# A grouped 1x1 convolution on one core: five chunk stores split into 112 rows and four times four rows

## The chip, the core and the metric

The kernel runs on one core of a Trainium2 chip. The core has compute engines with queues of their own: TensorE (PE, with its weight loads shown as PEld), VectorE (DVE), ScalarE (ACT) and GpSimd (POOL). SyncE (SP) issues DMAs. Sixteen DMA engines, numbered 0 to 15, move data between HBM and the on-chip memory SBUF; TensorE writes its results to PSUM. Work is ordered by semaphores, which an instruction or a finished DMA raises and another instruction waits for.

The metric is the time of one execution on the device in microseconds. A comparison of this kernel can tell differences of about 0.5%.

## The reference

The input x is an image of 512 x 512 pixels with 192 channels in bfloat16, the weights w are 1 x 1 x 4 x 48 x 48. The channels are in four groups of 48, and within a group each pixel's 48 values are multiplied by that group's 48 x 48 matrix:

```python
G, Cg = 4, 48
xg = x.reshape(B, H, W, G, Cg)
out = jnp.einsum('bhwgc,gcd->bhwgd', xg, w[0, 0])   # k is 1, so one tap and no padding
return out.reshape(B, H, W, 192)
```

It reads 100.66 MB of x and writes 100.66 MB of output.

## The kernel before

The 262,144 pixels are cut into 33 chunks. The first 28 and three of the tail have 64 pixels per partition, the last two have 32 (`PPC`, `TAIL`). A chunk of 64 lies as 128 rows, one per SBUF partition, and each row is a contiguous run of 64 x 192 bfloat16 values (24,576 bytes) in HBM. `rows_view` (L101) gives this view of input and output, so that a chunk is loaded by one DMA and stored by one DMA of 3072 KB. Four buffers hold loaded chunks (`x_sb`) and four hold chunks to be stored (`o_sb`, `NB` = 4); chunk n uses buffer n % 4.

SyncE issues the loads (L156). The load of chunk n waits until TensorE has transposed all of chunk n - 4 (`t_done`, L155).

TensorE works on groups of four pixels per partition, sixteen groups to a chunk of 64. For a group it makes six transposes into PSUM (L188) and six matmuls (L210) with a block-diagonal arrangement of the weights that is built once at the start (L174, L232). Before the first group of a chunk it takes 16 from the load's semaphore (L184), which a load raises to 16 when it has landed. The transposes run `LOOK` = 2 groups ahead of the matmuls. Most groups run inside a hardware loop over four chunks at a time; the five tail chunks are written out.

VectorE copies each group's transposes from PSUM to SBUF (L238), and in five groups of sixteen (`SHARE`) also one half of the matmul results (L245). ScalarE copies the matmul results, whole (L279) or the other half (L276), into `o_sb`. Both wait, before their first result of chunk n, for the complete store of chunk n - 4 (L242, L268), since it reads the same buffer. The amount waited for is taken from `st_total`, which counts 16 for each store DMA on that buffer's semaphore.

ScalarE also issues the stores, from its own queue and in program order with its copies. When a chunk's last copy is made, the store is put on the list `pending`, and it is issued two groups later (one in the tail) by `store` (L255 to L263). At the end ScalarE waits for all stores (L286).

Of the kernel before, what the change touches and what calls it, by code (L numbers as in the profile page):

```python
# [11 lines left out]
C = GROUPS * CG  # L12
# [12 lines left out]
PPC = 64  # L25
NB = 4
TAIL = (64, 64, 64, 32, 32)
NXP = 4
NOB = 4
NXS = 4  # L30
# [18 lines left out]
def shared(g):  # L49
    return (g % PERIOD) in SHARE  # L50


def bass_standalone__grouped__vision_kernel(nc, x, w, out):
# [4 lines left out]
    per_part = npix // 128  # L58
    mid = per_part - sum(TAIL)
    assert mid > 0 and mid % (NB * PPC) == 0  # L60
    n_mid = mid // PPC
    trips = n_mid // NB
    sizes = [PPC] * n_mid + list(TAIL)
    n_chunks = len(sizes)

    xf = x.rearrange("b h w c -> (b h w) c")
    of = out.rearrange("b h w c -> (b h w) c")
# [14 lines left out]
    body = NB * PPC // 4  # L82
    assert body % NXP == 0 and body % PERIOD == 0 and L1 == body * trips
    assert not shared(-1) and not shared(-2)
# [10 lines left out]
    def actT_cnt(g):  # L95
        return g - GT + 1

    def dveT_cnt(g):
        return sum(1 for h in range(GT, g + 1) if shared(h))

    def rows_view(ap, n):  # L101
        s = sizes[n]
        return ap[pix0[n]:pix0[n] + 128 * s, :].rearrange("(p i) c -> p (i c)", p=128)

    st_total, acc = [], [0] * NB
    for n in range(n_chunks):
        acc[n % NB] += 16
        st_total.append(acc[n % NB])

    def st_before(n):  # L110
        return st_total[n - NB] if n >= NB else 0

    with ExitStack() as es:
        block = es.enter_context(nc.Block())
        x_sb = [es.enter_context(nc.sbuf_tensor(f"x_sb{i}", [128, PPC * C], BF16)) for i in range(NB)]
        o_sb = [es.enter_context(nc.sbuf_tensor(f"o_sb{i}", [128, PPC * C], BF16)) for i in range(NB)]
# [4 lines left out]
        wt = es.enter_context(nc.sbuf_tensor("wt", [128, WCOLS], BF16))  # L121
        xT_ps = es.enter_context(nc.psum_tensor("xT_ps", [128, NXP, 1024], BF16))
        o_ps = es.enter_context(nc.psum_tensor("o_ps", [128, NOB, 512], F32))

        def sem(name):
            return es.enter_context(nc.semaphore(name))

        ld_sem = [sem(f"ld{i}") for i in range(NB)]
        st_sem = [sem(f"st{i}") for i in range(NB)]
# [6 lines left out]
        @block.gpsimd  # L136
        def _(gp):
            gp.memset(esel[:], 1.0).then_inc(p0_sem, 1)  # L138
            gp.memset(ident[:], 1.0).then_inc(p1_sem, 1)  # L139
            gp.wait_ge(p0_sem, 1)  # L140
            gp.affine_select(out=esel[:], in_=esel[:], pattern=[[-1, ECOLS]],  # L141
                             compare_op=AluOpType.is_equal, fill=0.0, base=ESHIFT,
                             channel_multiplier=1).then_inc(e_sem, 1)
            gp.wait_ge(p1_sem, 1)
            gp.affine_select(out=ident[:], in_=ident[:], pattern=[[-1, 128]],  # L145
                             compare_op=AluOpType.is_equal, fill=0.0, base=0,
                             channel_multiplier=1).then_inc(id_sem, 1)
# [13 lines left out]
        def _(pe):  # L161
# [16 lines left out]
            def transposes(g):  # L178
# [7 lines left out]
                for j in range(6):  # L186
                    col = lg * 2 * UC + j * 128
                    last = pe.transpose(xT_ps[:, g % NXP, j * 128:(j + 1) * 128],  # L188
                                        x_sb[b][:, col:col + 128], ident[:])
# [39 lines left out]
        def _(dve):  # L229
# [4 lines left out]
            for (op, g) in dve_prog:  # L234
                n, lg = groups[g]
                if op == "ev1":
                    wq.wait(t_done, g + 1)
                    dve.tensor_copy(xT_sb[g % NXS][:], xT_ps[:, g % NXP, 0:2 * UC]).then_inc(ev1_sem, 1)  # L238
                else:
# [9 lines left out]
        @block.scalar  # L249
        def _(act):  # L250
            wq = Waiter(act)
            act.sem_inc(act_sem, 2)
            pending = []

            def store(n):  # L255
                b = n % NB
                g = g1[n] - 1
                if g < GT:
                    wq.wait(mm_done, g + 3)
                else:  # L260
                    wq.wait(actT_sem, actT_cnt(g))
                    wq.wait(ev2T_sem, dveT_cnt(g))
                act.dma_start(rows_view(of, n), o_sb[b][:, 0:sizes[n] * C]).then_inc(st_sem[b], 16)  # L263

            for g in range(NG):
                n, lg = groups[g]
                if lg == 0:
                    wq.wait(st_sem[n % NB], st_before(n))  # L268
                wq.wait(mm_done, g + 1)
                while pending and pending[0][1] <= g:  # L270
                    store(pending.pop(0)[0])
                v = (2 * g) % NOB
                ob = o_sb[n % NB]
                if shared(g):
                    u = lg * 2
                    ins = act.copy(ob[:, u * UC:(u + 1) * UC], o_ps[:, v, 0:UC])  # L276
                else:
                    dst = ob[:, lg * 2 * UC:(lg + 1) * 2 * UC].rearrange("p (u c) -> p u c", u=2)
                    ins = act.copy(dst, o_ps[:, v:v + 2, 0:UC])  # L279
                ins.then_inc(act_sem if g < GT else actT_sem, 1)  # L280
                if g == g1[n] - 1:
                    pending.append((n, g + 2 if g < GT else g + 1))
            for (n, _) in pending:
                store(n)
            for b in range(NB):
                act.wait_ge(st_sem[b], acc[b])  # L286
# [28 lines left out]
```

## Time and profile before

| What | Value |
|---|---|
| Runs | 491.99, 489.92 and 491.54 us; median 491.54 |
| Profiled execution, its own time | 492.02 us |
| Span of that execution, first to last instruction | 490.3 us |
| Mean granted TensorE clock | 0.956 |
| Chunk loads: 31 of 3072 KB and 2 of 1536 KB, first and last issue | 0.8 and 426.2 us |
| Chunk stores: 31 of 3072 KB and 2 of 1536 KB, first and last issue | 31.4 and 474.0 us |
| One issue of a store on ScalarE's queue, median | 338 ns |
| Store, issue to landing, least / median / most | 15.9 / 40.3 / 45.6 us |
| Load, issue to landing, least / median / most | 10.0 / 38.4 / 45.6 us |

The profile shows one execution. The span runs from the first to the last instruction that was recorded. "Busy" counts an engine's own work and leaves out waiting and issuing. The DMA share is the mean busy share of the sixteen DMA engines, and GB/s is what they moved together in a stretch, counted by packets that start in it. A wait names the instruction that waited, what released it, and the microseconds. PEq is TensorE's sequencer: L165 there is the place where it takes from a semaphore. A DMA counts as landed when its last DMA engine has reported.

### The profile page before, as it was taken

The numbers are of one execution on the slowest core, as the hardware profiler recorded it, in microseconds if no ns is written. First come the engines' busy times: TensorE is split into PE (matmuls) and PEld (weight loads), VectorE is DVE, ScalarE is ACT, GpSimd is POOL, SyncE is SP. The second block draws the span as 40 slices with busy tenths as digits, with TensorE's granted clock in tenths as the row PEclk, the third lists the DMA queues.
The fourth block names the chain that finished last, engine by engine and source line by source line (L and its number), as shares of the span: only waits on it lengthen the run. The fifth ranks groups of instructions, "written<-read, shape, count | busy, mean of one in ns | idle before, by whom it ended". The sixth has DMA issues, their size and how long they took to land. (4 is left out here: it accounts for less than half of the span.)

```text
span 490.3 us, 14833 instructions
## 1 busy us (share of the span) xinstructions
PE 416.1 (85%) x6154; PEld 402.6 (82%) x6154; DVE 349.4 (71%) x673; ACT 348.8 (71%) x513; POOL 1.3 (0%) x8
## 2 busy tenths in 40 slices
PE   0987898999999999979897998977997979979850
PEld 0976798999999999979887888877987879979740
DVE  0766677888888888868676776766885767858740
ACT  1676687888888888867675776766785767858650
POOL 1000000000000000000000000000000000000000
PEclk9999899999999999999898998999998999989985
DMA  8999999999999999999999999999999999999760
GB/s 354 429 404 429 428 419 430 433 425 437 426 437 428 433 429 433 430 433 429 431 428 431 429 435 428 433 429 433 431 430 431 432 431 433 426 430 432 305 286 39
DMA packets 9736, 201.65 MB, mean 411 GB/s; under 512 B 1264, under 2 KB 1264, under 8 KB 1264
## 3 DMA queue, kind: packets, MB, share of 16 engines
q1 hardware_dynamic: 4960, 100.68, 48.2%
q10 hardware_dynamic: 4752, 100.67, 48.0%
q8 instruction: 13, 0.21, 0.2%
q14 instruction: 11, 0.09, 0.0%
HBM read 100.68 MB, written 100.66 MB: 411 GB/s over the span
## 5 line engine op out<-in xcount | busy, mean ns | idle before, releaser
L279 ACT CAST o_sb<-o_ps 128x768 bf16<-128x768 f32 x352 | 274.5, 798 | 114.2 <-PE o_ps L210 76.0
L238 DVE COPY xT_sb<-xT_ps 128x768 bf16<-128x768 bf16 x512 | 283.9, 554 | 87.9 <-PE xT_ps L188 79.1
L210 PE MATMUL o_ps<-wt,xT_sb 128*128 128x144 bf16 (+1 forms) x3072 | 305.9, 237 | 39.9 <-PEq L165 29.0
L188 PE MATMUL xT_ps<-ident,x_sb 128*128 128x128 bf16 x3072 | 263.5, 224 | 6.0 <-issue 4.0
L210 PEld LDWEIGHTS o_ps<-wt,xT_sb 128*128 128x128 bf16 x3072 | 216.0, 99 | 52.3 <-issue 37.2
L188 PEld LDWEIGHTS xT_ps<-ident,x_sb 128*128 128x128 bf16 x3072 | 203.7, 100 | 6.9 <-issue 6.6
L245 DVE CAST o_sb<-o_ps 128x384 bf16<-128x384 f32 x160 | 88.5, 553 | 23.3 <-DMA out_dram<-o_sb 20.5
L276 ACT CAST o_sb<-o_ps 128x384 bf16<-128x384 f32 x160 | 76.6, 479 | 10.1 <-PE o_ps L210 6.4
L174 PE MATMUL o_ps<-w_sb,esel 48*128 48x48 bf16 x10 | 0.6, 211 | 11.1 <-DMA w_sb<-in_w_dram 11.1
L174 PEld LDWEIGHTS o_ps<-w_sb,esel 48*128 48x128 bf16 x10 | 0.5, 113 | 11.1 <-issue 11.1
L232 DVE CAST wt<-o_ps 128x480 bf16<-128x480 f32 x1 | 0.7, 657 | 11.7 <-PE o_ps L174 11.7
L279 ACT ACT_TABLE_LOAD x1 | 1.3, 1283 | 0.9 <-PEq L300 0.9
L141 POOL TENSOR_SCALAR_AFFINE_SELECT esel<-esel 48x272 bf16<-48x272 bf16 x1 | 0.4, 405 | 0.0
L138 POOL MEMSET esel<- 48x272 bf16 x1 | 0.3, 318 | 0.3 <-POOLq L300 0.3
L145 POOL TENSOR_SCALAR_AFFINE_SELECT ident<-ident 128x128 bf16<-128x128 bf16 x1 | 0.3, 285 | 0.0
L139 POOL MEMSET ident<- 128x128 bf16 x1 | 0.2, 198 | 0.0
L300 POOL MEMSET const-bfloat16-1.0<- 128x1 bf16 x1 | 0.1, 101 | 0.0
L300 POOL MEMSET const-uint8-127<- 128x1 uint8 x1 | 0.1, 101 | 0.0
L300 POOL MEMSET const-float32-0.0<- 128x1 f32 x1 | 0.1, 98 | 0.3 <-issue 0.3
L300 POOL MEMSET const-float32-1.0<- 128x1 f32 x1 | 0.1, 98 | 0.0
## 6 DMA issues: line engine op xcount, KB each, us to landing
x_sb<-in_x_dram SPq DMA_DIRECT2D x31, 3072.0 KB, 38.2
out_dram<-o_sb ACTq DMA_DIRECT2D x31, 3072.0 KB, 40.7
x_sb<-in_x_dram SPq DMA_DIRECT2D x2, 1536.0 KB, 39.4
out_dram<-o_sb ACTq DMA_DIRECT2D x2, 1536.0 KB, 17.3
w_sb<-in_w_dram SPq DMA_DIRECT2D x1, 18.0 KB, 9.8
```

The costliest lines, as they stand in the source:

```text
L138: gp.memset(esel[:], 1.0).then_inc(p0_sem, 1)
L141: gp.affine_select(out=esel[:], in_=esel[:], pattern=[[-1, ECOLS]], compare_op=AluOpType.is_equal, fill=0.0, base=ESHIFT, channel_multipli ...
L145: gp.affine_select(out=ident[:], in_=ident[:], pattern=[[-1, 128]], compare_op=AluOpType.is_equal, fill=0.0, base=0, channel_multiplier=1) ...
L174: last = pe.matmul(o_ps[:, NOB - 1, col:col + CG], lhsT=esel[:, s0:s0 + 128], rhs=w_sb[:, g, :], start=True, stop=True, skip_group_check=True)
L188: last = pe.transpose(xT_ps[:, g % NXP, j * 128:(j + 1) * 128], x_sb[b][:, col:col + 128], ident[:])
L210: last = pe.matmul(o_ps[:, v, c0:c1], lhsT=xs[:, j * 128:(j + 1) * 128], rhs=wt[:, WOFF[tc]:WOFF[tc] + (c1 - c0)], start=(tc == 0), stop=( ...
L232: dve.tensor_copy(wt[:], o_ps[:, NOB - 1, 0:WCOLS]).then_inc(wc_sem, 1)
L238: dve.tensor_copy(xT_sb[g % NXS][:], xT_ps[:, g % NXP, 0:2 * UC]).then_inc(ev1_sem, 1)
L245: dve.tensor_copy(o_sb[n % NB][:, u * UC:(u + 1) * UC], o_ps[:, (2 * g + 1) % NOB, 0:UC]).then_inc(ev2_sem if g < GT else ev2T_sem, 1)
L276: ins = act.copy(ob[:, u * UC:(u + 1) * UC], o_ps[:, v, 0:UC])
L279: ins = act.copy(dst, o_ps[:, v:v + 2, 0:UC])
L300: nc = _bacc.Bacc("TRN2", target_bir_lowering=False, num_devices=1)
```

## The change

In the stores of chunks 4, 10, 16, 22 and 28 the one DMA of 128 rows becomes five DMAs: one of rows 0 to 111, and four of four rows each, 112 to 115 up to 124 to 127. A DMA of 112 rows is made by all sixteen DMA engines, seven rows each; a DMA of four rows is made by engines 0 to 3, one row each. All five are issued one after another from ScalarE's queue at the place of the one store. Each raises the buffer's semaphore by 16, so the totals waited for grow by 80 instead of 16 for these chunks. The other 28 stores, all loads and all computation stay as they are.

```diff
+RELIEF = (4, 10, 16, 22, 28)
+PARTS = ((0, 112), (112, 116), (116, 120), (120, 124), (124, 128))
...
+    def store_parts(n):
+        return PARTS if n in RELIEF else ((0, 128),)
+
     st_total, acc = [], [0] * NB
     for n in range(n_chunks):
-        acc[n % NB] += 16
+        acc[n % NB] += 16 * len(store_parts(n))
         st_total.append(acc[n % NB])
...
-                act.dma_start(rows_view(of, n), o_sb[b][:, 0:sizes[n] * C]).then_inc(st_sem[b], 16)
+                dst = rows_view(of, n)
+                for (r0, r1) in store_parts(n):
+                    act.dma_start(dst[r0:r1, :], o_sb[b][r0:r1, 0:sizes[n] * C]).then_inc(st_sem[b], 16)
```

## The prediction

> **What bounds the kernel now.** I read the page first, for what each resource does over the span.
>
> ```profile
> span 490.3 us, 14833 instructions
> PE 416.1 (85%) x6154; PEld 402.6 (82%) x6154; DVE 349.4 (71%) x673; ACT 348.8 (71%) x513; POOL 1.3 (0%) x8
> ...
> DMA  8999999999999999999999999999999999999760
> ...
> DMA packets 9736, 201.65 MB, mean 411 GB/s; under 512 B 1264, under 2 KB 1264, under 8 KB 1264
> ...
> out_dram<-o_sb ACTq DMA_DIRECT2D x31, 3072.0 KB, 40.7
> ```
>
> No compute engine is full, while the sixteen DMA engines are busy in every slice but the last three. A store lands 40.7 us after its issue although a chunk comes about every 15 us, so several transfers are always queued. Then I cut the busy time by stretches, above all at the end (the columns after the five engines are the granted clock, the DMA share and GB/s).
>
> ```profile
> 100.00:200.00 100.00, 100.00 (x1535) 96.57 (x1533) 86.35 (x168) 87.08 (x129) 0.00 (x0) 1.00 1.00 431
> 200.00:440.00 240.00, 206.81 (x3027) 201.34 (x3025) 172.47 (x332) 170.62 (x253) 0.00 (x0) 0.95 1.00 431
> ...
> 474.00:478.80 4.80, 0.00 (x0) 0.00 (x0) 0.00 (x0) 0.00 (x0) 0.00 (x0) 0.59 0.79 333
> 478.80:482.00 3.20, 0.00 (x0) 0.00 (x0) 0.00 (x0) 0.00 (x0) 0.00 (x0) 0.50 0.05 23
> 482.00:486.00 4.00, 0.00 (x0) 0.00 (x0) 0.00 (x0) 0.00 (x0) 0.00 (x0) 0.50 0.06 28
> 486.00:489.50 3.50, 0.00 (x0) 0.00 (x0) 0.00 (x0) 0.00 (x0) 0.00 (x0) 0.50 0.06 25
> ```
>
> From 478.8 to 489.5 us the share is 0.05 to 0.06, one sixteenth: a single DMA engine works alone for 10.7 us while fifteen are done. So the end is set by one late engine. Its mean rate is 12.6 MB (201.65 MB over 16) in 487.7 us (the first packet starts at 1.8), 25.8 GB/s; the others run at (431 - 25.8) / 15 = 27.0 GB/s. One row of a chunk is 24,576 B (3072 KB over 128 rows), so a row takes 0.95 us on the late engine and 0.91 us on another. The completion records show the delay grow: at the store of chunk 4 the last of the sixteen engines is 4.2 us behind the first, at chunk 16 12.9, at chunk 28 19.9, while the other fifteen mostly stay within 3 us of each other.
>
> Last, the waits between 210 and 440 us:
>
> ```profile
> ACT o_sb L279 <- DMA out_dram<-o_sb: 34.3, 15, 3.4
> ...
> PE o_ps L210 <- PEq L165: 28.1, 13, 2.8
> ```
>
> The columns are microseconds in total, times, longest. ScalarE waits for a store to leave its buffer, TensorE for a load (L165). Both counts need all sixteen engines, so both waits end with the late one.
>
> **The change, part by part.** In five stores every engine gets 7 rows (112 / 16) where it had 8, and engines 0 to 3 get 4 more, one per four-row part: 11. Over the kernel an engine moves 512 row-equivalents (12.6 MB / 24,576 B); engines 4 to 15 lose 5, engines 0 to 3 gain 15.
>
> *The late engine, if it is one of 4 to 15.* It has work queued without a break to the end, so five rows fewer bring its end forward by 5 x 0.95 = 4.75 us, from 489.5 to 484.75.
>
> *Engines 0 to 3, by count alone.* They gain 15 x 0.91 = 13.65 us. What they can absorb: 10.7 us after 478.8, and before it the idle shares of the stretches from 440 us on (440:445 to 474:478.8 gave 1.02, 0.99, 0.95, 0.44, 0.94, 0.77, 0.56 and 0.79) make 7.3 us of sixteen engines, 7.8 of fifteen. Together 18.5 us. An average engine of the four would end at 489.5 - 18.5 + 13.65 = 484.65. The four are not equal: offsets of the fifteen at the last load run from 0 to 5.5 us, mostly 0 to 2.5, so the latest of four lies about 1.5 us past the average: 486.1. By count alone the end moves from 489.5 to 486.1, -3.4 us, set by the later of two nearly equal ends. Engines 0 to 3 have only 3.4 us over, spread on 20 four-row parts 0.17 us each.
>
> *The price of a four-row part.* Nothing in the trace of before moves four neighbouring rows alone; every big transfer spreads 128 rows on sixteen engines. Low end: each of the four engines takes its row in the usual 0.91 us, extra 0; a smaller one is excluded, since no row at full length in the trace took less. High end: the four rows lie next to each other in SBUF and go one after another through whatever way serves them, 4 x 0.91 = 3.65 us, extra 2.74 for each part, 20 x 2.74 = 54.8 us. That rows can stretch each other is in the trace, in the stretch from 33 to 37 us:
>
> ```profile
> 30.00:33.00 3.00, 2.86 (x46) 2.67 (x44) 2.53 (x5) 2.58 (x4) 0.00 (x0) 1.00 1.01 434
> 33.00:37.00 4.00, 4.00 (x62) 3.71 (x59) 3.24 (x8) 3.29 (x6) 0.00 (x0) 1.00 0.95 330
> 37.00:60.00 23.00, 17.50 (x254) 16.79 (x254) 14.32 (x28) 14.57 (x21) 0.00 (x0) 0.97 1.01 432
> ```
>
> At 330 GB/s a row took 0.91 x 431 / 330 = 1.19 us on average. That was a general stretch; here four engines go for four adjacent rows at the same moment, four times over, with a load row of their other queue between. Between ends a factor of four apart I take the geometric middle, 1.82 us, which says that each row waits for one other: extra 0.91, times 20, 18.2 us on engines 0 to 3. Ends kept: 0 and 54.8.
>
> [...] No run here shows a store of four rows.
>
> *The 112-row part* shifts which rows an engine reads. Extra from 0 (its rows are as long) to 0.28 us a row by the 1.19 us stretch, 35 rows an engine, 9.8 us on all engines. I take 0: all sixteen engines are in it, as in the rows of 0.91. The 9.8 stays for the range.
>
> *ACT's queue.* Twenty more issues at 338 ns (the store issue's row) are 6.8 us, 1.35 in each of five stores. Behind them in program order stand ScalarE's evictions (L279), and TensorE waits for those. At chunks 4 and 10 (issues at 90.9 and 166.2 us) TensorE is full, 100.00 of 100, so it may lose 1.35 us each time, and SP's next load issue with it. It costs nothing, because that load lands 38 us after its issue behind queued loads and the DMA share stays 1.00. At chunks 16, 22 and 28 the cover is the 34.3 us ScalarE waits in 210 to 440 us. Without that cover the price is 5 x 1.35 = 6.8 us.
>
> *The semaphore totals* (80 in place of 16 for five stores) change no order: ScalarE (L268) and VectorE (L242) still wait for all of chunk n-4. Queued behind that wait are the evictions and the pending store of chunk n-1. Late engines 0 to 3 would end it in place of the late one.
>
> **Sum.** 486.1 + 18.2 = 504.3 us for the last landing. The span ran 0.8 past it and the profiled execution 1.7 past that (492.02 against 490.3), so 506.8; it stood 0.5 above the median of the runs, 491.54. Predicted 506.3, say 506 us.
>
> **The rivals.**
> *It gains (ends faster).* If a four-row part costs no more than its rows, the end is 486.1: 491.54 - 3.4 = 488.1 us, at best 486.8 when the late engine sets it. For it: at 431 GB/s all sixteen engines ran side by side for 340 us. Against it: engines 0 to 3 have but 0.17 us per part before the gain is gone; nearly all of the interval from 0 to 2.74 lies beyond.
> *The late engine is one of 0 to 3.* It then gains 15 rows, 15 x 0.95 = 14.3 us: 505.8 us. No view tells which engine is late; by count 4 of 16. [...]
> *The 112-row part stretches everywhere:* 9.8 - 4.75 = +5 us at most without the four-row price, 496.6 us.
>
> **How the numbers follow.** This kernel's runs span 0.4%, so about 0.5%, 2.5 us, can be told from no change. Four-row parts that wait: 0.46 (0.04 of it within 0.5%, where the wait is some 0.05 to 0.3 us a part). Parts at row price with a relieved late engine: 0.36, of which 0.09 within 0.5% because the latest of engines 0 to 3 lies 3 us or more past the average. Late engine among 0 to 3: 0.14. The 112-row stretch or an uncovered ACT queue: 0.04, slower. Faster 0.27, same 0.13, slower 0.60. The two largest cases have different signs. Slower's own range is 495 to 542. The range reaches down to the gain's 486.5, and up to 530, an extra of 2.1 us a part, past which I leave 0.1.
>
> **What would show it.** The stretches at the end: a DMA share near 0.25 means that engines 0 to 3 finish last, 0.06 one engine as now. From issue to landing the five relieved stores would take well longer than their neighbours, L279's wait for out_dram would grow, and GB/s would fall below 431 in steps after 91 us. If the share at the end stays 0.06 with the end near 485, the four-row price was wrong and the gain holds; if 0.06 with an end near 504, the late engine was among the four.

## The result

The changed kernel is slower: the ratio of its time to the time of before is 1.048, with a 95% interval from 1.042 to 1.054. The median of its six runs is 518.81 us against 489.94 us for before. Three of the six were disturbed; the other three took 511.11, 514.89 and 515.97 us. The profiled execution is the one of 511.11 us, with a span of 509.3 us where before had 490.3.

These lines are from the page of the changed kernel (busy time, DMA slices, queues):

```profile
span 509.3 us, 14853 instructions
PE 415.8 (82%) x6154; PEld 401.6 (79%) x6154; DVE 348.7 (68%) x673; ACT 349.0 (69%) x513; POOL 1.3 (0%) x8
...
DMA  8999999999999999999999999799999997996775
...
DMA packets 9816, 201.65 MB, mean 396 GB/s; under 512 B 1344, under 2 KB 1344, under 8 KB 1344
```

The compute engines have the same busy time as before (PE 415.8 against 416.1 us), and the bytes are the same. What fell is the mean DMA rate, from 411 to 396 GB/s. The 80 new packets under 512 B are completion counts: five stores times four new parts times four engines. So a four-row part is made by four engines; the trace does not give their numbers.

The stretches answer to those shown of before:

```profile
100.00:200.00 100.00, 96.53 (x1482) 93.25 (x1480) 83.36 (x163) 83.77 (x124) 0.00 (x0) 1.00 1.00 423
200.00:440.00 240.00, 189.60 (x2797) 183.84 (x2795) 158.58 (x306) 158.27 (x234) 0.00 (x0) 0.90 0.97 403
440.00:500.00 60.00, 51.80 (x763) 50.06 (x760) 43.13 (x84) 43.98 (x66) 0.00 (x0) 0.94 0.81 325
500.00:504.00 4.00, 0.00 (x0) 0.00 (x0) 0.00 (x0) 0.09 (x1) 0.00 (x0) 0.71 0.85 352
504.00:506.00 2.00, 0.00 (x0) 0.00 (x0) 0.00 (x0) 0.00 (x0) 0.00 (x0) 0.50 0.32 135
506.00:509.00 3.00, 0.00 (x0) 0.00 (x0) 0.00 (x0) 0.00 (x0) 0.00 (x0) 0.50 0.05 20
```

Read the two last columns together. From 100 to 200 us the DMA engines are as busy as before (1.00) but move 423 GB/s where they moved 431: their rows take longer. From 200 to 440 us they move 403 at a share of 0.97: rows take longer, and engines now also run dry. By 440 us this is 100 x (1 - 423/431) + 240 x (1 - 403/431) = 17.5 us of transfer behind. The tail from 440 us on has more to move and does it at 325 GB/s.

The waits show where the engines ran dry:

```profile
PE o_ps L215 <- PEq L170: 56.2, 15, 13.8
ACT o_sb L286 <- DMA out_dram<-o_sb: 51.0, 10, 13.9
DVE o_sb L250 <- DMA out_dram<-o_sb: 42.2, 8, 13.0
```

Between 210 and 440 us ScalarE's wait for a store to leave its buffer was fifteen waits of 1.3 to 3.4 us. Now three of ten in the whole run are 12.81, 13.89 and 12.77 us long. They are the waits for the split stores of chunks 10, 16 and 22, whose buffers chunks 14, 20 and 26 need. From issue to the last completion those stores took 53, 55 and 54.5 us (ends at 220.86, 319.57 and 414.41 us); the store of chunk 10 had taken 37.6 us before. In ScalarE's timeline the last of the three, and the stretches around it:

```profile
414.41 0.80 ACT L286 CAST o_sb<-o_ps 128x768 bf16<-128x768 f32 x1 [12.77 <-DMA out_dram<-o_sb]
```

```profile
406.00:414.40 8.40, 0.00 (x0) 0.00 (x0) 0.00 (x0) 0.00 (x0) 0.00 (x0) 0.50 0.87 375
414.40:419.70 5.30, 4.35 (x37) 4.30 (x38) 2.61 (x5) 3.25 (x5) 0.00 (x0) 0.50 0.93 399
419.70:430.00 10.30, 10.30 (x162) 10.05 (x160) 8.80 (x18) 8.53 (x14) 0.00 (x0) 1.00 0.73 291
```

All compute stands still to 414.40 us, then TensorE runs at a granted clock of 0.50 for 5.3 us, and while it catches up the DMA share sinks to 0.73: between the load at 398.87 us and the one at 425.99 us a single transfer was issued, the store at 414.41 us.

From the packet records one can split each span into three: the time the bytes need at 912 ns a row (the median row), the stretching of rows beyond that, and idle time, each as a mean over the sixteen DMA engines. Before: 467.8 + 5.0 + 17.5 us. After: 467.8 + 17.1 + 24.4. Of the 19.0 us lost, 12.1 are stretched rows and 6.9 idle engines. Several runs below are given in these terms.

The completion counts of each store show how far the engines lie apart. At the store of chunk 5, the first behind a split, the four latest engines are 6.6, 9.3, 10.6 and 13.8 us behind the first, where before one was 4.9 and the others at most 2.8 behind. Three more rows make 2.7 us of it; the rest is stretched rows.

### The profile page after: what moved, and what is told of

Same layout as the page of the kernel before. It is cut to its first block, busy times and chain, and to the rows that moved or that the text cites. A ratio compares the mean times of both kernels' runs of the same rounds, so it can differ in the third digit from the quotient of the medians.

```text
span 509.3 us, 14853 instructions
## 1 busy us (share of the span) xinstructions
PE 415.8 (82%) x6154; PEld 401.6 (79%) x6154; DVE 348.7 (68%) x673; ACT 349.0 (69%) x513; POOL 1.3 (0%) x8
## 5 line engine op out<-in xcount | busy, mean ns | idle before, releaser
L283 ACT CAST o_sb<-o_ps 128x384 bf16<-128x384 f32 x160 | 76.6, 479 | 18.9 <-PE o_ps L215 9.3
L179 PE MATMUL o_ps<-w_sb,esel 48*128 48x48 bf16 x10 | 0.6, 209 | 11.5 <-DMA w_sb<-in_w_dram 11.5
L179 PEld LDWEIGHTS o_ps<-w_sb,esel 48*128 48x128 bf16 x10 | 0.5, 111 | 11.5 <-issue 11.5
L237 DVE CAST wt<-o_ps 128x480 bf16<-128x480 f32 x1 | 0.7, 657 | 12.1 <-PE o_ps L179 12.1
## 6 DMA issues: line engine op xcount, KB each, us to landing
out_dram<-o_sb ACTq DMA_DIRECT2D x2, 1536.0 KB, 11.5
```

The costliest lines, as they stand in the source:

```text
L179: last = pe.matmul(o_ps[:, NOB - 1, col:col + CG], lhsT=esel[:, s0:s0 + 128], rhs=w_sb[:, g, :], start=True, stop=True, skip_group_check=True)
L237: dve.tensor_copy(wt[:], o_ps[:, NOB - 1, 0:WCOLS]).then_inc(wc_sem, 1)
```

## The experiments

Three theories stood at the start. Adjacency: four engines that read four adjacent rows at once stretch each other, as in the prediction. Count: three more rows on four engines hold the buffer too long, whatever their length. Third: the 112-row part itself costs. The diffs of this part are shortened to what differs.

### The short parts in other shapes

Every fourth row for a part, in place of four adjacent rows:

```diff
-PARTS = ((0, 112), (112, 116), (116, 120), (120, 124), (124, 128))
+PARTS = ((0, 112, 1), (112, 128, 4), (113, 128, 4), (114, 128, 4), (115, 128, 4))
```

> The four-row parts take every fourth row (112, 116, 120, 124, then 113 and so on) in place of four adjacent rows; row counts per DMA engine and the five issues stay. Adjacency theory (four engines that read adjacent rows at once stretch each other): the four-row rows fall from the 1.3 to 4.3 us seen in the changed kernel to about 0.91 us, the three waits of 12.8, 13.9 and 12.8 us on a store shrink to under 6 us each, and the time falls to 488 to 495 us. Count theory (three more rows in one store on four engines, each alternating with a load row, hold the buffer too long): waits and time stay, 511 to 520 us, whatever the rows' own length.

Measured: ratio 1.044 (1.037 to 1.051), median 513.5 us. Stretch 17.5 and idle 27.3 us per engine. The time did not move and a long wait for a store stayed (16.6 us), as the count theory said; but the stretch stayed too, and more rows alone do not explain that. At the store of chunk 5 the four latest engines are only 3.7 to 5.3 us behind the first, against 6.6 to 13.8 with adjacent rows: adjacency does delay them, but this is not what sets the time.

One part of 16 rows, one row on every engine:

```diff
+PARTS = ((0, 112), (112, 128))
```

> The five stores become 112 rows and one part of 16 rows, which all sixteen engines make with one row each; every engine has 8 rows per store again. Count theory: within 0.5% of the kernel before, since no engine has more rows. Adjacency theory: the sixteen adjacent rows are stretched too, by up to 2.7 us in each of five stores on every engine, 490 to 504 us, with single store rows above 1.3 us. If the 112-row part itself is what costs (its rows spread differently over the engines): 496 us or more, with long rows before the 16-row part.

Measured: ratio 1.044 (1.040 to 1.048), median 511.9 us. Stretch is 15.3 and idle 24.5 us per engine. Here every engine has eight rows a store by count (112 / 16 and one more), as before the change, and the loss is the same within the intervals. So unequal counts are not needed for it: the count theory is out as the explanation. Two stretches over the splits of chunks 10 and 16:

```profile
186.00:202.00 16.00, 15.99 (x249) 15.51 (x247) 13.94 (x29) 13.80 (x21) 0.00 (x0) 1.00 1.00 401
274.00:291.00 17.00, 8.29 (x122) 8.00 (x120) 6.84 (x14) 6.86 (x11) 0.00 (x0) 0.78 1.00 377
```

At a full share the rate is 401 and 377 GB/s in place of 431. The packet records show rows of up to 5.35 us from 274 us on, before the first count of the 112-row part had landed (283.2 us), so within that part. Late in this run two engines lag (16.1 and 31.4 us behind the first at the store of chunk 27, the other fourteen at most 5.0) although by count all have the same rows.

Two parts of eight rows, on eight engines each by the author's count:

```diff
+PARTS = ((0, 112), (112, 120), (120, 128))
```

> The five stores become 112 rows and two parts of eight adjacent rows, so engines 0 to 7 have 9 rows and 8 to 15 have 7. Count theory: the store rows that pile up on one engine fall from 3 to 1 per store, no long wait is left; 485 us if the late engine is among 8 to 15, 495 us if it is among 4 to 7. Adjacency theory: the parts' rows are still stretched, by about as much per part as in the changed kernel but in 10 parts instead of 20: 497 to 505 us.

Measured: ratio 1.044 (1.040 to 1.047), median 513.4 us. The same loss with a third distribution of the 16 rows, and more than either theory gave. It does not tell in which half the late engine is, since the common cost covers it.

Two stores of 120 and 8 rows:

```diff
+RELIEF = (8, 20)
+PARTS = ((0, 120), (120, 128))
```

> Only the stores of chunks 8 and 20 are split, into 120 rows and 8 rows. If 120 rows are made by fifteen engines with eight rows each, the sixteenth engine has 16 rows less over the kernel and engines 0 to 7 have two more. If the late engine is that sixteenth one, its end comes 16 x 0.95 = 15 us earlier and the time falls to 478 to 485 us. If it is another, it keeps its rows or gains two: 490 to 493 us.

Measured: ratio 1.016 (1.012 to 1.021), median 497.7 us. After the split of chunk 8 one engine's counts land 7.2 us ahead of all others (217.8 us against 225.0 for the store of chunk 12), eight rows of 0.91 us, so 120 rows are made by fifteen engines and one is left out. The late engine is still there, 11.9 us behind the first of the others: the one left out is not the late one. Two such splits cost 7.3 us, above both forecasts, and rows of up to 4.3 us stand where the 120-row part ran. Over the two splits (155 to 175 and 335 to 352 us) the rate is 400 and 399 GB/s at a full share.

### The 112-row part alone, and a cut along the other axis

Rows 112 to 127 left out, and, in a second run, a cut along the columns:

```diff
+PARTS = ((0, 112),)
```

```diff
+h = sizes[n] * C // 2
+for k in (0, 1):      # in the five chunks; all 128 rows, half of the columns each
+    act.dma_start(dst[:, k * h:(k + 1) * h], o_sb[b][:, k * h:(k + 1) * h])
```

> In the five chunks only rows 0 to 111 are stored; rows 112 to 127 of those chunks are left out of the output. Theory A (the 112-row store itself stretches rows, because its seven rows per engine fall on other partitions than the eight of a 128-row store): although every engine has five rows less, store rows above 1.1 us appear in five clusters and the time is 494 to 508 us. Theory B (only the short parts of 4, 8 or 16 adjacent rows stretch): no such clusters, every engine 4.6 us less work, 484 to 487 us.

> The same five chunks are stored by two DMAs each, but cut along the columns: all 128 rows, 12,288 B of each row, twice. Every engine keeps the rows of a 128-row store. Theories A and B (which rows an engine reads decides): no stretched rows, 489 to 493 us. Theory C (it is the cutting into several DMAs that costs, through issue, completion or more semaphore counts): at least a quarter of the lost 22 us comes back, 495 us or more.

Measured: with 112 rows only, ratio 1.022 (1.016 to 1.029), median 503.28 us, although every engine has by count five rows, 4.6 us, less to do. The measured loss is 11.7 us against the median of before in that comparison, 491.61. If the rows left out would have saved their 4.6 us, the 112-row part costs 16.3 us, an estimate. The stretches over the splits of chunks 10 and 16:

```profile
183.00:202.00 19.00, 18.43 (x286) 17.75 (x283) 16.06 (x32) 15.83 (x25) 0.00 (x0) 1.00 1.01 393
274.00:292.00 18.00, 9.66 (x114) 9.22 (x111) 6.16 (x13) 6.43 (x10) 0.00 (x0) 0.72 1.00 381
```

and the same stretches in the kernel before:

```profile
183.00:202.00 19.00, 19.00 (x296) 18.49 (x295) 16.57 (x33) 16.55 (x25) 0.00 (x0) 1.00 1.01 432
274.00:292.00 18.00, 16.80 (x264) 16.38 (x261) 14.74 (x30) 14.65 (x22) 0.00 (x0) 1.00 1.00 431
```

All DMA engines are busy in both, but move 393 and 381 GB/s in place of 432 and 431. 176 store rows are over 1.03 us where before had 11. The delay falls on all engines, but on two of them most: at the store of chunk 23 two are 26.1 and 30.3 us behind the first and the others at most 13.2, where before one was 17.5 and the others at most 4.7 behind.

The run does not separate what makes the rows longer. By count an engine makes seven rows in place of eight, which rows these are no trace names, and whether the SBUF or the HBM side decides was tested only for the four-row parts below.

The cut along the columns: ratio 1.003 (1.001 to 1.005), median 492.75 us. Twice the DMAs for the same five stores, and nearly nothing lost:

```profile
100.00:200.00 100.00, 96.37 (x1481) 93.17 (x1479) 83.37 (x163) 83.82 (x124) 0.00 (x0) 1.00 1.01 429
200.00:440.00 240.00, 199.79 (x2985) 194.21 (x2983) 168.67 (x326) 168.90 (x248) 0.00 (x0) 0.93 1.00 426
```

```profile
ACT o_sb L287 <- DMA out_dram<-o_sb: 44.0, 11, 9.9
```

A little stretch is left (8.4 us per engine against 5.0), and 2.1 us less idle time make up for most of it. So two DMAs in place of one, with larger semaphore totals, cost next to nothing. The second fence is as telling: this kernel waits 44.0 us for stores, up to 9.9 at a time, close to the 51.0 of the changed kernel, and loses 0.3%. The DMA share stays 1.00 there: read together, a wait on a buffer costs when DMA engines run dry by it.

### The four-row parts alone, SBUF side and HBM side

In four runs, with one trace each, rows 0 to 111 of the five chunks are left out, so only the length of the parts' rows counts. The parts read adjacent or every fourth partition, and write adjacent or every fourth row of the output:

```diff
+act.dma_start(dst[112:116, :],   o_sb[b][112:116, ...])     # both adjacent
+act.dma_start(dst[112:128:4, :], o_sb[b][112:128:4, ...])   # both strided
+act.dma_start(dst[112:116, :],   o_sb[b][112:128:4, ...])   # SBUF strided, HBM adjacent
+act.dma_start(dst[112:128:4, :], o_sb[b][112:116, ...])     # SBUF adjacent, HBM strided
```

> In the five chunks only the four parts of four adjacent rows (112 to 127) are stored; rows 0 to 111 of those chunks are left out of the output, so the time is far less for that reason and says nothing. To be read is the length of the 20 parts' rows on engines 0 to 3. Theory B, and the prediction's middle: 1.8 us on average, up to 3.65. Theory A with harmless short parts: 0.91 to 1.0 us.

> As the run with only the four-row parts, again without rows 0 to 111 of the five chunks, but each part takes every fourth row. Adjacent rows as the cause: 0.91 to 1.0 us a row here against 1.8 or more with adjacent rows. Four engines on four rows as such as the cause: the same long rows as with adjacent ones.

> As the runs with only the four-row parts (rows 0 to 111 of the five chunks are left out), but each part reads every fourth partition of SBUF and writes four adjacent rows of the output, so that those rows land in a permuted order. SBUF side as the cause: the rows of chunks 4 and 10 stay at 0.91 us, as with strided parts (at most one over 1.03). HBM side as the cause: a dozen or more of the 32 are over 1.03 us, as with adjacent parts.

> The reverse: each part reads four adjacent partitions and writes every fourth row of the output (again permuted, and rows 0 to 111 left out). SBUF side as the cause: a dozen or more of the 32 rows of chunks 4 and 10 are over 1.03 us, up to 2.7. HBM side as the cause: at most one.

Measured, store rows over 1.03 us while the parts of chunks 4 and 10 ran (90 to 112 and 164 to 215 us): adjacent partitions 17 and 15 (HBM adjacent, HBM strided), every fourth partition 1 and 1. Before has none there. In these two places it is the partitions of SBUF that decide, not the rows of HBM. The stretch from 182 to 195 us, first before the change and then in the four runs, in the order of the diff:

```profile
182.00:195.00 13.00, 13.00 (x204) 12.57 (x201) 11.20 (x23) 11.35 (x17) 0.00 (x0) 1.00 1.00 431
```

```profile
182.00:195.00 13.00, 12.96 (x200) 12.38 (x198) 11.14 (x23) 11.34 (x17) 0.00 (x0) 1.00 1.02 420
```

```profile
182.00:195.00 13.00, 13.00 (x203) 12.56 (x201) 11.28 (x22) 11.35 (x17) 0.00 (x0) 1.00 1.03 442
```

```profile
182.00:195.00 13.00, 13.00 (x203) 12.57 (x201) 11.27 (x23) 11.39 (x18) 0.00 (x0) 1.00 1.01 433
```

```profile
182.00:195.00 13.00, 12.98 (x202) 12.54 (x200) 11.25 (x23) 11.03 (x18) 0.00 (x0) 1.00 1.01 403
```

420 and 403 GB/s with adjacent partitions, 442 and 433 with strided ones, at nearly the same share; 431 before. In the run with adjacent rows the long rows of both stretches have 15.8 us in excess of 0.912 us; if all of them are the parts' own rows, that is 0.49 for each of the 32, 1.40 us a row. From 215 us on long rows no longer tell the runs apart (42, 38, 31 and 31 in the order of the diff). The completion counts still do: at the store of chunk 17, behind three splits, the four latest engines are 13.4 to 20.3 and 11.5 to 22.0 us behind the first with adjacent partitions, 7.5 to 10.7 and 6.5 to 9.3 us with every fourth one.

The prediction's high end, an estimate, has the four rows of a part go one after another, 4 x 0.91 = 3.65 us. These rows took 1.40 us on average by the sum above, 2.7 us at most in the run with adjacent rows on both sides and 4.6 at most in the one with adjacent partitions alone, so 3.65 us is no fixed price here.

### Other cuts: 64 rows, and loads

```diff
+PARTS = ((0, 64), (64, 128))
```

> The five stores become two parts of 64 adjacent rows; every engine makes four rows of each part, eight in all. Theory A (any store of other than 128 rows gives the engines other partitions than their usual ones, and engines that read the same ones stretch each other): stretched store rows in all five places, an excess of 100 us or more over all rows, and 500 to 515 us. If only parts whose row count is not a power of two, or the short parts, do it: no stretched rows, 489 to 493 us.

Measured: ratio 1.022 (1.014 to 1.031), from runs of 496.07, 497.85, 504.56 and 522.59 us; the first was profiled. More stretch than in the changed kernel (18.9 us per engine against 17.1; 257 store rows over 1.03 us), but only 7.6 us idle against 24.4. So it is not 112 rows as such that stretches. Its DMA engines stay fed: from 440 to 480 us their share is 0.91 to 1.02, where the changed kernel's falls to 0.66 and 0.58 from 460 to 480. Why was not tried.

Nine loads of 112 and 16 rows, the stores as before:

```diff
+for (r0, r1) in ((0, 112), (112, 128)) if n % NB == 0 else ((0, 128),):
+    sp.dma_start(x_sb[b][r0:r1, ...], src[r0:r1, :]).then_inc(ld_sem[b], 16)
```

> Stores as before; nine loads (chunks 0, 4, 8 and so on) are made as 112 rows and 16 rows. If the stretching lies in which partitions an engine touches, whether it reads or writes: stretched load rows in nine places and a loss near nine fifths of the 22 us of the like cut of five stores, 515 to 535 us. If only reads of SBUF stretch each other: no long load rows beyond those of before, 489 to 494 us.

Measured: ratio 1.072 (1.065 to 1.079), median 526.05 us, 35.9 us over before; nine fifths of 22 us would be 39.6. From 12 us on, load rows over 1.03 us rise from 51 to 666; over the whole run store rows, which are not cut here, rise from 11 to 319. At a full share the rate falls:

```profile
100.00:200.00 100.00, 98.26 (x1505) 94.67 (x1503) 84.66 (x166) 85.49 (x125) 0.00 (x0) 1.00 1.01 405
```

So cut loads stretch rows like cut stores. No run pointed to a version faster than before.

## Why the prediction was right, and where it was not

*Direction and range: right.* Slower at 0.60; 518.81 us and every single run lie in 486.5 to 530. The point, 506 us, was too low, and that it came so near is in part luck: 18.2 us put on the four-row parts stand where the 112-row part, taken as nothing, cost most.

*What bounds the kernel: right as far as shown.* The transfers bound it, and every loss came with less GB/s. That the late engine is among 4 to 15 fits, but is not shown: at the store of chunk 11 four engines of the changed kernel are 17.7 to 27.1 us behind the first, and two others 6.1 and 6.4 (before, the one late engine was 9.5). Which it is stays open; the 120-row run excludes the engine left out there.

*"Engines 0 to 3, by count alone": the count did not set the time.* With equal counts (16-row part) the loss is the same within the intervals. The gain of 3.4 us could not show, because the cost beside it is several times as large.

*"The price of a four-row part": the mechanism right, the size open.* Taken as 1.82 us a row, measured 1.40 us in the first two places of the run where they stand alone, so 0.49 extra; if the other parts are alike, times 20, 9.8 us in place of 18.2. Beside a 112-row part the price was higher: at the store of chunk 5 the four latest engines are some 6 us later than with every fourth row, about 1.5 us for each of the four parts. Adjacency is shown to delay the four engines, on the SBUF side; but every fourth row, without that delay at first, lost as much time, so this price did not set it. The 542 us at the far end of the slower range has 54.8 us extra for the 20 parts, 2.74 us each; no run shows that price.

*"The 112-row part ... I take 0": this step failed.* The reason given was that all sixteen engines are in it, as in the rows of 0.91 us. They are (sixteen completion counts for each such part, as for 128 rows; by count seven rows each in place of eight), and the rows still became longer. Alone it lost 11.7 us with less to move, 16.3 us by the estimate above, more than even the 9.8 us that was kept for the range. It is the largest part of the loss, and it is not tied to the four engines of the short parts. The rival "the 112-row part stretches everywhere", with 0.04 shared, was the main one. Some 7 us are left between it and the 23.5 of all parts together (0.048 x 490). Adding 9.8 for the four-row parts and taking off the 3.4 of the count would nearly fill this, but with every fourth row and with 16 rows, where 23.1 and 21.5 us were lost, a like gap is left, so it stays open.

*"ACT's queue ... costs nothing": nearly.* Five issues took 2.18 us at chunk 10 (1.69 by the row used), and no view shows a cost of it. At chunk 28 they took 3.91 us and ScalarE's next copy waits for them, on the chain that ended last; there the named cover, the wait for a store, was not to be had, and it cost up to 4 us there:

```profile
453.97 3.91 ACTq L270 DMA_DIRECT2D out_dram<-o_sb  x5
457.92 0.80 ACT L286 CAST o_sb<-o_ps 128x768 bf16<-128x768 f32 x1 [4.11 <-issue]
```

*"The semaphore totals change no order", with engines 0 to 3 ending the wait: right, but not priced.* The sum moved ends of DMA work about and left out that a wait of 13 us lets the DMA engines run dry; idle engines are 6.9 of the 19.0 us. The column cut shows that a wait of 9.9 us can still be free.

*What would show it:* the rate did fall in steps after 91 us. The share at the end was 0.32 for 2 us and then 0.05, not 0.25 to the end: one engine alone landed last, at 508.9 us, 2.7 us behind the next, and fourteen had landed by 505.3. The last store was issued only at 500.12 us, since compute, delayed by the store of chunk 22 at 414.41 us, had become the last chain (PE 13% of it against 1% before).

*The late engine among 0 to 3:* no run shows it, and none excludes it. The numbers 0 to 3 themselves no run shows; they stand for the four engines that make a four-row part. That these are the same four each time is read from the completion counts of the changed kernel: the four latest engines are 6.6 to 13.8 us behind the first after one split (chunk 5), 17.7 to 27.1 after two (chunk 11) and 26.1 to 36.2 after three (chunk 17), the other twelve at most 3.0, 6.4 and 11.9.

## What to carry to other kernels

A DMA that keeps all sixteen engines busy is not yet a full-rate DMA: here transfers of 128 rows ran at 431 GB/s beside each other, and stretches with cuts along the rows (112 alone, 112 with 16, 120 with 8, 64 with 64, four adjacent rows) at 377 to 421, for loads and stores alike. Four rows of every fourth partition, alone, ran at 433 and 442. If such a transfer must be cut, cut its columns and keep the 128 rows: that cost 0.3% here. To tell stretched transfers from missing ones, read the DMA share and GB/s side by side: a share of 1.00 with fewer GB/s was stretch here (423 in place of 431 from 100 to 200 us), a lower share starvation (0.87 with 375 from 406 to 414.4 us), and only then look which wait starved it.

## What the runs showed of the hardware that was not expected

- One DMA engine of sixteen is slower in company. Between 100 and 440 us some 6% of the rows before the change are longer than the others' 0.912 us, stores mostly 0.97 to 1.0 and loads about 0.93; about one in sixteen, they are read as its rows. Alone at the end it takes 0.912 too. The cause stays open.
- After each of the three stalls of some 13 us TensorE was granted half its clock for 4.3, 4.6 and 5.3 us more (0.50 up to 225.18, 324.16 and 419.74 us), so the work behind these waits started slowly.
- Four-row parts that take every fourth partition are slower to issue: median 602 ns each, in both runs that do, against 319 and 325 with adjacent partitions. Every fourth row of HBM alone does not do it.
- A single row of 24,576 B took up to 5.4 us in the 112-row store alone, six times its usual 0.91.
